# Two z1 tiles that stay on chip, an earlier load of the others, and small steps moved apart in a one-core gated mix of attention and gMLP

## The chip, the cores and the metric

The kernel runs on one core of a Trainium2 chip. A core has TensorE (PE: matmuls, with its own weight loads, PEld), VectorE (DVE), ScalarE (ACT), GpSimd (POOL) and SyncE (SP), each with an instruction stream of its own that it works off in order, and 16 DMA engines that serve the queues. An instruction waits on semaphores until what it reads is there and what it overwrites has been read. SBUF, the on-chip memory, has 128 partitions; PSUM, into which matmuls write, is used here as 8 banks of 512 f32 per partition. The metric is the device time of one execution in microseconds (us), median over runs.

## What is computed

x is 2048 x 1024, in bf16. Branch A is attention with 32 heads of 32: each position s looks at the 8 positions s, s-2, ..., s-14 of its own head. Branch B is a gMLP: a projection to 2 x 1792 columns, GELU, a layer norm of one half, a product with a 2048 x 2048 matrix over the positions, a product with the other half, and a projection back. A gate per position mixes them.

```
g = sigmoid((x * gate_w).sum(-1, keepdims=True))
qkv = x @ wqkv                                  # 32 heads of 32
logits = q . k[s - 2w], w = 0..7, * 32**-0.5    # positions below 0: -1e9
a = (softmax(logits) . v[s - 2w]) @ wo
z = gelu(x @ w_in);  z1, z2 = z[:, :1792], layernorm(z[:, 1792:])
b = (z1 * (w_sp @ z2 + b_sp[:, None])) @ w_out
out = g * a + (1 - g) * b
```

## The kernel before, in words

**Stages of TensorE**, one after the other (line of the matmul in brackets): part of z2 (L280), q, k and v (L516), the rest of z2 (L280), z1 (L591), the product with w_sp for the position chunks 0 and 1 (L605), the same for chunks 2 and 3 by seven products in place of eight (L696), the projections back, where w_out's products (L822) alternate with wo's (L899 for the first pair of row blocks, then L909, seven products in place of eight as well). Everything that those shortened schemes add and subtract is kept in range by powers of two, below.

**z1.** 14 tiles of 128 features (f) by 4 chunks of 512 positions (c). Each (f, c) takes 8 matmuls into one bank; ScalarE applies the GELU into a staging slot (`z1s`, two slots, taken in turn), and after four chunks SP stores the tile to DRAM (`z1_d`, L595). `load_z1c(0)` (L466) fetches chunk 0 with its 14 tiles into `z1c_slots[0]`; it is called after the z1 loop. Chunk 1 goes into `z1c_slots[1]`, which lies over the staging slots; chunks 2 and 3 are fetched tile by tile in the seven products (L710). `z1c_slots[0]` lies over the buffers of the "looks", below; the place of its tiles 12 and 13 does not.

**The w_sp products of chunks 0 and 1** (`g_chunk`). For each f, 16 matmuls into one bank, a ScalarE copy to one of three slots (L609), a bias added by VectorE (L612) and the product with z1 (L613), which is the first reader of the loaded z1.

**Attention** runs on VectorE beside all this, by 8 groups of 4 heads: products of q and k (L327) folded down (L330, L333, L338, L341), the maximum over the 8 windows by one `tensor_reduce` (L348) and the subtraction (L349), the exponential on ScalarE (L352), the sum over the windows by another `tensor_reduce` (L355), reciprocal (L356), weights (L357), the products with v (L365) and their folds (L371, L372, L368). The products with v of group g - 1 stand between the steps of group g. Loads of q, k and v per group and the store of the output (`store_o`, L383) are on SP's queue.

**The order of the work.** The engines' orders are written out at build time. A counter of planned time, `beat`, advances with each group of matmuls; what is registered with `beat.at(t, ...)` is emitted when the counter passes t, and the steps of attention are emitted by a plan that adds up durations given in the code (`yield t, 1.4, soft_a`). These times decide places in the order alone; on the chip an instruction runs when its engine has come to it and its waits are over.

**Looks and powers.** Sums of absolute values are taken of w_out (7 parts) and wo (4 parts): SP loads a part (L572) and ScalarE sums it (L574), during the z1 stage, planned every 8 us. From each set of sums a power of two is made by `whole_power`, in three turns: VectorE cuts the exponents (L546 to L549); TensorE transposes that column (L553) and VectorE takes its maximum (L554); TensorE spreads it over the partitions by a small matmul (L556) and VectorE forms the factors (L557 to L563). The turns of w_out's power are planned 70 us into the z1 stage, and 12 and 24 us into the w_sp stage; those of wo's at 42, 60 and 80 us.

**Rows of w_sp** 8 to 15 (128 rows each) are loaded on ScalarE's queue, summed (L625), scaled by powers of two per row (L662), stored to DRAM (`wsp_d`, L663) and read back transposed by SP (L463) in time for the seven products, whose sums t1 to t4 VectorE makes (L670 to L676). The scaled biases take a matmul (L653), a ScalarE copy (L655) and a store and load on SP.

**The first pair of row blocks** of the last stage (`mix_pair(0)`) is followed by `wo_scale` (L856), which scales all of wo by its power, by four sums of wo (L864 to L870) and by `attn_pair(0)` (L899). On VectorE, `mix_pair` has two steps near its end (L848, L850).

Of the kernel before, what the change touches and what calls it, by code (L numbers as in the profile page):

```python
# [15 lines left out]
P = 128  # L16
# [8 lines left out]
W = 8  # L25
# [32 lines left out]
def kernel(  # L58
# [78 lines left out]
    v_up = sm.tile([P, 1], I32, name="v_up")  # L137
    back = sm.tile([P, 1], I32, name="back")
    att_L = sm.tile([P, 2 * W * 8 * HG], F32, name="att_L")
    att_m = sm.tile([P, 2, 1, 32], F32, name="att_m")  # L140
    att_r = sm.tile([P, 2, 1, 32], F32, name="att_r")
    att_A = sm.tile([P, 2 * W * 8 * HG], BF, name="att_A")

# [174 lines left out]
    TT = nc.vector.tensor_tensor  # L318

    q4 = q_t.rearrange("p (n d) -> p n d", d=4)  # L320
    by_window = L4.rearrange("p a w n -> p a n w")

    def qk_steps(jh):
        def mul():
# [15 lines left out]
    def to_one():  # L340
# [3 lines left out]
        for t in range(3):  # L344
            nc.gpsimd.memset(_sub_ap(first, 128 + 32 * t, [[128, 2], [1, 24 - 8 * t]]), NEG)

    def soft_a():
        nc.vector.tensor_reduce(att_m[:, :, 0, :], by_window, AX.X, ALU.max)  # L348
        TT(L4, L4, att_m[:].to_broadcast([P, 2, W, 32]), ALU.subtract)  # L349

    def soft_exp():
        nc.scalar.activation(L[:], L[:], ACT.Exp, scale=float(SCALE))  # L352

    def soft_b():
        nc.vector.tensor_reduce(att_m[:, :, 0, :], by_window, AX.X, ALU.add)  # L355
        nc.vector.reciprocal(att_r[:], att_m[:])  # L356
        TT(A4, L4, att_r[:].to_broadcast([P, 2, W, 32]), ALU.mult)  # L357

    def pv_steps(g, jh):
# [30 lines left out]
    def attention_steps(t):  # L390
        beat.at(t - 8.0, lambda: load_qk(0))
        beat.at(t + 35.0, lambda: load_v(0))
        for g in range(NG):
            for took, fn in qk_steps(0) + qk_steps(1) + [(1.2, to_two), (1.1, to_one)]:
                yield t, took, fn
            t = beat.vector
            if g + 1 < NG:
                beat.at(t + 1.0, lambda g=g: load_qk(g + 1))
            if g == 0:
                t += 3.0  # L400
            else:
                for took, fn in pv_steps(g - 1, 0):
                    yield t, took, fn
                t = beat.vector
            yield t, 1.4, soft_a
            t = beat.vector
            beat.at(t + 1.0, soft_exp)
            if g == 0:
                t += 5.0
            else:  # L410
                for took, fn in pv_steps(g - 1, 1):
                    yield t, took, fn
                t = beat.vector
                if g + 1 < NG:
                    beat.at(t + 1.0, lambda g=g: load_v(g))
                else:
                    load_v(g)
                if g % 2 == 0:
                    beat.at(t + 1.5, lambda g=g: store_o(g - 1))
            yield t, 2.0, soft_b  # L420
            t = beat.vector
        for took, fn in pv_steps(NG - 1, 0) + pv_steps(NG - 1, 1):
            yield t + 5.0, took, fn
        t = beat.vector
        beat.at(t + 14.0, lambda: store_o(NG - 1))
# [37 lines left out]
        sync.dma_start_transpose(wsp_slots[c][:, :, aa, :], src)  # L463

    def load_z1c(c):
        sync.dma_start(z1c_slots[c % 2].rearrange("p f t -> p (f t)"), z1_d[c])  # L466

    tc_order = ctx.enter_context(tc.manual_schedule())

# [98 lines left out]
    for k in range(11):  # L568
        slot = look_slots[k % 2]
        src = wout_v[:, 2 * k:2 * k + 2, :] if k < 7 else wo_rows[:, 2 * k - 14:2 * k - 12, :]  # L570
        total = w_l1[:, k:k + 1] if k < 7 else wo_l1[:, k - 7:k - 6]
        beat.at(beat.now + 3.0 + 8.0 * k, lambda src=src, slot=slot: sync.dma_start(  # L572
            slot.rearrange("p (f n) -> p f n", f=2), src))
        beat.at(beat.now + 10.5 + 8.0 * k, lambda total=total, slot=slot: nc.scalar.activation(  # L574
            look_out, slot, ACT.Abs, accum_out=total))

    for g in range(NG):
        beat.at(beat.now + 6.0 + 10.0 * g, lambda g=g: turn_wo(g))
    w_steps = whole_power(w_up, omg[:])
    beat.at(beat.now + 70.0, lambda: (nc.vector.tensor_reduce(top[:], w_l1[:], AX.X, ALU.max), next(w_steps)))  # L580

    for f in range(NF):
        ch = f // 4
        w1 = w1_slots[ch % 2]
        if f % 4 == 0 and ch in (1, 2):
            load_w1(ch + 1)
        z1s = z1s_slots[f % 2]
        for c in range(4):
            ps = psum.tile([P, 512], F32, name="ps", tag="ps")
            for kt in range(KT):  # L590
                nc.tensor.matmul(ps[:], w1[:, kt, (f % 4) * P:(f % 4 + 1) * P], xT[:, kt, 512 * c:512 * (c + 1)],  # L591
                                 start=(kt == 0), stop=(kt == KT - 1))
            nc.scalar.activation(z1s[:, c, :], ps[:], ACT.Gelu_apprx_tanh)  # L593
            beat.run(KT * 512)
        sync.dma_start(z1_d[:, :, f * 512:(f + 1) * 512].rearrange("c p t -> p c t"), z1s)  # L595

    gs = [0]

# [159 lines left out]
    def w_tiles(f):  # L758
        return (w_out_sb[:, f, 0:512], w_out_sb[:, f, 512:1024],
                w_out_sb[:, f + 7, 0:512], w_out_sb[:, f + 7, 512:1024])  # L760
# [63 lines left out]
    def mix_slot(a, n0):  # L824
        return mix_slots[2 * (a % 4) + n0 // 512]

    def mix_pair(q):
        a, b = 2 * q, 2 * q + 1
        s = row_pair_sums[q % 2]
        og = [omg[:, r:r + 1] for r in (a, b)]  # L830
        stt = nc.vector.scalar_tensor_tensor
        act = nc.scalar.activation
        pa = bank()
        product7(pa, u_rows(q, 0, 0), lambda j: w_tiles(f_of(q, j))[0], True)
        pb = bank()
        nc.scalar.copy(pb[:], pa[:])
        pe = bank()
        product7(pe, s[0], lambda j: w_t(f_of(q, j), 0), True)
        for r in (1, 0):
            act(mix_slot(a + r, 512), pe[:], ACT.Copy, scale=og[r])  # L840
        product7(pb, s[1], lambda j: w_t(f_of(q, j), 1), False)
        pc = bank()
        nc.scalar.copy(pc[:], pb[:])
        product7(pa, u_rows(q, 0, 1), lambda j: w_tiles(f_of(q, j))[2], False)
        act(mix_slot(a, 0), pa[:], ACT.Copy, scale=og[0])
        o_scale(a)
        product7(pb, s[2], lambda j: w_t(f_of(q, j), 2), False)
        stt(mix_slot(b, 512), pb[:], og[1], mix_slot(b, 512), ALU.mult, ALU.add)  # L848
        product7(pc, s[3], lambda j: w_tiles(f_of(q, j))[3], False)
        stt(mix_slot(a, 512), pc[:], og[0], mix_slot(a, 512), ALU.mult, ALU.add)  # L850
        product7(pb, u_rows(q, 1, 1), lambda j: w_t(f_of(q, j), 3), False)
        act(mix_slot(b, 0), pb[:], ACT.Copy, scale=og[1])
        o_scale(b)

    def wo_scale():
        nc.vector.tensor_scalar(wo_sb, wo_sb, wo_up[:].bitcast(F32), None, ALU.mult)  # L856

    def wo_tiles():
        return wo_sb[:, 0:4, 0:512], wo_sb[:, 0:4, 512:1024], wo_sb[:, 4:8, 0:512], wo_sb[:, 4:8, 512:1024]
# [160 lines left out]
        for k in range(4):  # L1020
            u_sum(q, k)

    load_z1c(0)
    t0 = beat.now
    for r in range(8):
        beat.at(t0 + 3.5 * r, lambda r=r: natural(r))
# [21 lines left out]
    biases()  # L1048
    wo_steps = whole_power(wo_up, g_s[:])
    for k in range(2):  # L1050
        beat.at(t0 + 12.0 + 12.0 * k, lambda: next(w_steps))
        beat.at(t0 + 60.0 + 20.0 * k, lambda: next(wo_steps))
    beat.at(t0 + 42.0, lambda: (nc.vector.tensor_reduce(top[:], wo_l1[:], AX.X, ALU.max), next(wo_steps)))
    g_chunk(0)
    g_chunk(1)
    for n in range(7):
# [3 lines left out]
    u_steps = whole_power(u_up, omg[:, 8:16])  # L1060
    prepare(1)
    mix_pair(0)
    wo_scale()
    u_sums(6)
    for k in range(4):
        wo_sum(k)
# [38 lines left out]
```

## Time and profile before

| | us |
|---|---|
| runs | 701.94, 700.68, 703.32; median 701.94 |
| profiled execution, own time | 702.48 |
| its span | 700.4 |
| TensorE busy | 683.9 |
| VectorE, ScalarE busy | 531.5, 385.8 |
| mean granted TensorE clock | 0.993 |

Rows of the profile name a line, an engine, an operation and what it writes and reads. In a time line the first two columns are start and duration, and a bracket at the end gives the idle time of the engine ahead of the instruction and what ended it. In the view of waits the columns are total, number and longest. In the groups of instructions the columns behind the bar are busy time, mean duration in ns and idle time ahead. "SPq" is SP's queue at the issue of a DMA. `arena` is the one large SBUF buffer in which nearly all tiles lie, so a row's line tells more than its tile name; `z_d` is `z1_d`. Some matmul records are missing from a trace (439 of 448 in a group, for instance).

### The profile page before, as it was taken

What the parts mean: (1) busy time and instruction counts of PE and PEld (TensorE: products, weight loads), DVE (VectorE), ACT (ScalarE), POOL (GpSimd) and SP (SyncE); (2) the same over time, 40 slices, a digit from 0 to 9 for tenths busy, and PEclk for the clock granted to TensorE, in tenths of its full rate; (3) what the DMA queues carried; (4) which work ended last, traced back from release to release, by engine and by line L of the source; (5) the groups of instructions that cost most, each with busy time, mean ns of one, the idle gap of its engine ahead of it and who ended that gap; (6) DMA issues with size and microseconds to landing.
All of it is one profiled execution on the core that took longest, in us unless ns stands there. A gap on an engine that the chain in (4) does not pass through costs nothing.

```text
span 700.4 us, 8978 instructions
## 1 busy us (share of the span) xinstructions
PE 683.9 (98%) x3307; PEld 360.3 (51%) x3355; DVE 531.5 (76%) x652; ACT 385.8 (55%) x778; POOL 13.7 (2%) x44
## 2 busy tenths in 40 slices
PE   9999999999999999999999599999999989999998
PEld 4499666666665554444444244444444444444443
DVE  0004689999999999999993998267589998676663
ACT  4345544435568898666664797673665552232232
POOL 0000000000000101100000000000000000000000
PEclk9999999999999999999999799999999999999999
DMA  8996868768673233997777937946211323222220
GB/s 231 188 201 162 194 168 200 183 174 159 181 198 140 87 111 100 250 296 251 271 249 243 315 128 178 279 99 228 73 32 61 120 61 76 60 61 75 61 60 30
DMA packets 186923, 109.19 MB, mean 156 GB/s; under 512 B 145920, under 2 KB 171520, under 8 KB 186624
## 3 DMA queue, kind: packets, MB, share of 16 engines
q1 hardware_dynamic: 184576, 100.23, 53.2%
q10 hardware_dynamic: 2304, 8.39, 3.4%
q8 instruction: 26, 0.43, 0.2%
q14 instruction: 17, 0.14, 0.1%
HBM read 59.77 MB, written 34.67 MB: 135 GB/s over the span
## 4 chain that ended last, share of the span: by engine, by line
PE 81%; DMA 8%; ACT 4%; SPq 3%; DVE 2%; issue 2%; DVEq 0%; ACTq 0%
PE ps L516 24%; PE ps L280 14%; PE ps L696 12%; PE ps L822 12%; PE ps L605 11%; PE ps L909 6%; DMA z_d<-arena 4%; DMA arena<-in_B_w_out_dram 2%; PE ps L591 2%; SPq L463 2%; ACT arena L593 1%; ACT arena L574 1%; DMA arena<-z_d 1%; PE ps L899 1%; SPq L572 1%
## 5 line engine op out<-in xcount | busy, mean ns | idle before, releaser
L516 PE MATMUL ps<-arena 128*128 128x512 bf16 (+1 forms) x896 | 166.2, 349 | 0.0
L516 PEld LDWEIGHTS <-arena 128*128 128x128 bf16 x896 | 120.3, 144 | 45.8
L327 DVE TENSOR_TENSOR arena<-arena 128x8192 bf16<-128x8192 bf16 x16 | 70.7, 4421 | 56.2 <-DMA arena<-k_d 56.0
L519 ACT CAST arena<-ps 128x512 bf16<-128x512 f32 (+1 forms) x112 | 57.7, 526 | 85.7 <-PE ps L516 80.5
L605 PE MATMUL ps<-arena 128*128 128x512 bf16 x439 | 100.0, 387 | 0.5
L280 PE MATMUL ps<-arena 128*128 128x512 bf16 (+1 forms) x501 | 97.0, 352 | 1.4 <-DMA arena<-in_B_w_in_dram 0.7
L591 PE MATMUL ps<-arena 128*128 128x512 bf16 x439 | 96.4, 379 | 0.5
L822 PE MATMUL ps<-arena 128*128 128x512 f16 (+1 forms) x380 | 91.2, 379 | 0.5
L696 PE MATMUL ps<-arena 128*128 128x512 f16 (+1 forms) x385 | 84.7, 379 | 0.6 <-issue 0.3
L605 PEld LDWEIGHTS <-arena 128*128 128x128 bf16 x448 | 44.0, 99 | 61.7 <-issue 11.7
L280 PEld LDWEIGHTS <-arena 128*128 128x128 bf16 x512 | 50.0, 98 | 48.1 <-issue 1.3
L591 PEld LDWEIGHTS <-arena 128*128 128x128 bf16 x448 | 43.8, 98 | 52.7
L365 DVE TENSOR_TENSOR arena<-arena,att_A 128x8192 bf16<-128x8192 bf16 x16 | 70.7, 4418 | 0.0
L822 PEld LDWEIGHTS <-arena 128*128 128x128 f16 (+1 forms) x392 | 38.3, 98 | 46.1
L696 PEld LDWEIGHTS <-arena 128*128 128x128 bf16 (+1 forms) x392 | 38.0, 98 | 45.9 <-issue 0.5
L330 DVE TENSOR_TENSOR arena<-arena 128x4096 bf16<-128x4096 bf16 (+1 forms) x32 | 56.2, 1757 | 1.0
L909 PE MATMUL ps<-arena 128*128 128x512 f16 (+3 forms) x200 | 50.3, 375 | 0.1
L285 ACT ACTIVATE arena<-ps 128x512 bf16<-128x512 f32 (+1 forms) x64 | 34.3, 538 | 26.8 <-PE ps L280 26.7
L889 DVE SCALAR_TENSOR_TENSOR arena<-ps,g_s,arena 128x512 bf16<-128x512 f32 (+2 forms) x33 | 23.9, 733 | 29.9 <-ACT arena L941 20.0
L593 ACT ACTIVATE arena<-ps 128x512 bf16<-128x512 f32 x56 | 31.2, 595 | 25.5 <-DMA z_d<-arena 12.6
L371 DVE TENSOR_TENSOR arena<-arena 128x4096 bf16<-128x4096 bf16 x16 | 36.6, 2289 | 0.4
L909 PEld LDWEIGHTS <-arena 128*128 128x128 f16 (+1 forms) x200 | 19.4, 98 | 23.1 <-issue 0.2
(168 smaller groups left out, 627.3 us busy)
## 6 DMA issues: line engine op xcount, KB each, us to landing
arena<-k_d SPq DMA_DIRECT2D x8, 960.0 KB, 7.9
arena<-v_d SPq DMA_DIRECT2D x8, 960.0 KB, 6.0
z_d<-arena SPq DMA_DIRECT2D x14, 512.0 KB, 3.6
arena<-in_A_wqkv_dram SPq DMA_DIRECT2D x24, 256.0 KB, 4.1
arena<-in_B_w_in_dram SPq DMA_DIRECT2D x4, 1024.0 KB, 5.6
q_d<-arena SPq DMA_DIRECT2D x32, 128.0 KB, 2.4
k_d<-arena SPq DMA_DIRECT2D x32, 128.0 KB, 2.2
arena<-q_d SPq DMA_DIRECT2D x8, 512.0 KB, 4.6
```

The costliest lines, as they stand in the source:

```text
L280: nc.tensor.matmul(ps[:, 0:N], xT[:, kt, i * P:(i + 1) * P], w2[:, kt, ZC * c:ZC * c + N], start=(kt == 0), stop=(kt == KT - 1))
L327: TT(prod.rearrange("p (w j c) -> p w j c", w=W, j=8, c=C), in0, in1, ALU.mult)
L330: return lambda: TT(pv[:, :, 0:half], pv[:, :, 0:half], pv[:, :, half:2 * half], ALU.add)
L365: TT(prod.rearrange("p (w j d h) -> p w j d h", w=W, j=8, d=DH, h=HG), in0, in1, ALU.mult)
L516: nc.tensor.matmul(ps[:, n0:n1].rearrange("p (t c) -> p t c", c=C), lhsT, wgt[:, pos0:pos1, kt, :], start=(kt == 0), stop=(kt == KT - 1))
L519: nc.scalar.copy(st[:, j % 4, n0:n1], ps[:, n0:n1])
L591: nc.tensor.matmul(ps[:], w1[:, kt, (f % 4) * P:(f % 4 + 1) * P], xT[:, kt, 512 * c:512 * (c + 1)], start=(kt == 0), stop=(kt == KT - 1))
L593: nc.scalar.activation(z1s[:, c, :], ps[:], ACT.Gelu_apprx_tanh)
L605: nc.tensor.matmul(ps[:], z2[:, f, i, :], wsp[:, i, :, :].rearrange("p a t -> p (a t)"), start=(i == 0), stop=(i == 15))
L696: nc.tensor.matmul(dst[:], lhs[:, k, :], rhs(k), start=first and k == 0, stop=k == 7, skip_group_check=not first)
L822: nc.tensor.matmul(dst[:], lhs[:, j, :], rhs(j), start=first and j == 0, stop=j == 6, skip_group_check=not first)
L909: nc.tensor.matmul(dst, lhs[:, k, :], rhs[:, k, :], start=first and k == 0, stop=k == 3, skip_group_check=not first)
```

## The change

- **z1.** For tiles 12 and 13 the GELU of chunks 0 and 1 writes to its place in `z1c_slots[c]`, and only chunks 2 and 3 go through the staging slot and to DRAM. `load_z1c` fetches tiles 0 to 11. For chunk 0 it is called after the store of tile 12.
- **Looks** every 7 us of planned time instead of 8, from 2 us instead of 3.
- **Turns of the powers**: w_out's at 72 us into the z1 stage, then 14 and 32 us into the w_sp stage; wo's at 48, 66 and 84 us.
- **wo** is scaled in two halves of its columns; the first stands between the two late VectorE steps of `mix_pair`, the second where the whole stood.
- **Windows**: maximum and sum over 8 windows by three folds of 256, 128 and 64 elements instead of one `tensor_reduce`; the planned durations of some attention steps change with it.

In the order of instructions that comes out, w_out's transposition stands behind 5 tiles of the w_sp product (before: 4) and its spreading matmul behind 10 (before: 7); wo's behind 20 and 25 (before: 18 and 24); the scaled biases' matmul stands behind 19 in both. On VectorE the first L612 and L613 stand behind L365, L371 and L372 of group 6 (before: behind L365). On SP the store of the attention's last output stands ahead of the last four transposes from `wsp_d` (before: behind two of them).

```diff
-    att_m = sm.tile([P, 2, 1, 32], F32, name="att_m")
+    att_m = sm.tile([P, 2, 4, 32], F32, name="att_m")
...
+    def windows(op):
+        TT(att_m[:], L4[:, :, 0:4, :], L4[:, :, 4:8, :], op)
+        TT(att_m[:, :, 0:2, :], att_m[:, :, 0:2, :], att_m[:, :, 2:4, :], op)
+        TT(att_m[:, :, 0:1, :], att_m[:, :, 0:1, :], att_m[:, :, 1:2, :], op)
+
     def soft_a():
-        nc.vector.tensor_reduce(att_m[:, :, 0, :], by_window, AX.X, ALU.max)
-        TT(L4, L4, att_m[:].to_broadcast([P, 2, W, 32]), ALU.subtract)
+        windows(ALU.max)
+        TT(L4, L4, att_m[:, :, 0:1, :].to_broadcast([P, 2, W, 32]), ALU.subtract)
...
     def soft_b():
-        nc.vector.tensor_reduce(att_m[:, :, 0, :], by_window, AX.X, ALU.add)
-        nc.vector.reciprocal(att_r[:], att_m[:])
+        windows(ALU.add)
+        nc.vector.reciprocal(att_r[:], att_m[:, :, 0:1, :])
...
-            for took, fn in qk_steps(0) + qk_steps(1) + [(1.2, to_two), (1.1, to_one)]:
+            for took, fn in qk_steps(0) + qk_steps(1) + [(0.7, to_two), (0.7, to_one)]:
...
-            yield t, 1.4, soft_a
+            yield t, 1.65, soft_a
...
-            yield t, 2.0, soft_b
+            yield t, 2.2, soft_b
...
     def load_z1c(c):
-        sync.dma_start(z1c_slots[c % 2].rearrange("p f t -> p (f t)"), z1_d[c])
+        sync.dma_start(z1c_slots[c][:, 0:12, :].rearrange("p f t -> p (f t)"), z1_d[c, :, 0:12 * 512])
...
-        beat.at(beat.now + 3.0 + 8.0 * k, lambda src=src, slot=slot: sync.dma_start(
+        beat.at(beat.now + 2.0 + 7.0 * k, lambda src=src, slot=slot: sync.dma_start(
             slot.rearrange("p (f n) -> p f n", f=2), src))
-        beat.at(beat.now + 10.5 + 8.0 * k, lambda total=total, slot=slot: nc.scalar.activation(
+        beat.at(beat.now + 9.5 + 7.0 * k, lambda total=total, slot=slot: nc.scalar.activation(
             look_out, slot, ACT.Abs, accum_out=total))
...
-    beat.at(beat.now + 70.0, lambda: (nc.vector.tensor_reduce(top[:], w_l1[:], AX.X, ALU.max), next(w_steps)))
+    beat.at(beat.now + 72.0, lambda: (nc.vector.tensor_reduce(top[:], w_l1[:], AX.X, ALU.max), next(w_steps)))
...
-            nc.scalar.activation(z1s[:, c, :], ps[:], ACT.Gelu_apprx_tanh)
+            keep = f > 11 and c < 2
+            nc.scalar.activation(z1c_slots[c][:, f, :] if keep else z1s[:, c, :], ps[:], ACT.Gelu_apprx_tanh)
             beat.run(KT * 512)
-        sync.dma_start(z1_d[:, :, f * 512:(f + 1) * 512].rearrange("c p t -> p c t"), z1s)
+        c0 = 2 if f > 11 else 0
+        sync.dma_start(z1_d[c0:4, :, f * 512:(f + 1) * 512].rearrange("c p t -> p c t"), z1s[:, c0:4, :])
+        if f == 12:
+            load_z1c(0)
...
         stt(mix_slot(b, 512), pb[:], og[1], mix_slot(b, 512), ALU.mult, ALU.add)
+        wo_scale(0)
         product7(pc, s[3], lambda j: w_tiles(f_of(q, j))[3], False)
         stt(mix_slot(a, 512), pc[:], og[0], mix_slot(a, 512), ALU.mult, ALU.add)
...
-    def wo_scale():
-        nc.vector.tensor_scalar(wo_sb, wo_sb, wo_up[:].bitcast(F32), None, ALU.mult)
+    def wo_scale(h):
+        half = wo_sb[:, :, 512 * h:512 * h + 512]
+        nc.vector.tensor_scalar(half, half, wo_up[:].bitcast(F32), None, ALU.mult)
...
-    load_z1c(0)
     t0 = beat.now
...
     for k in range(2):
-        beat.at(t0 + 12.0 + 12.0 * k, lambda: next(w_steps))
-        beat.at(t0 + 60.0 + 20.0 * k, lambda: next(wo_steps))
-    beat.at(t0 + 42.0, lambda: (nc.vector.tensor_reduce(top[:], wo_l1[:], AX.X, ALU.max), next(wo_steps)))
+        beat.at(t0 + 14.0 + 18.0 * k, lambda: next(w_steps))
+        beat.at(t0 + 66.0 + 18.0 * k, lambda: next(wo_steps))
+    beat.at(t0 + 48.0, lambda: (nc.vector.tensor_reduce(top[:], wo_l1[:], AX.X, ALU.max), next(wo_steps)))
...
     mix_pair(0)
-    wo_scale()
+    wo_scale(1)
```

The changed file's lines are shifted: L556 becomes L560, L613 becomes L621, L696 becomes L704, L899 becomes L909, for instance.

More of the change, by code (lines that the diff above doesn't have):

```diff
@@ L320 @@
     q4 = q_t.rearrange("p (n d) -> p n d", d=4)
-    by_window = L4.rearrange("p a w n -> p a n w")
     def qk_steps(jh):
```

## The prediction

> **What bounds the kernel now.** I read the page first, then who waited for whom, then time lines around the waits of TensorE (PE). The page:
>
> ```profile
> span 700.4 us, 8978 instructions
> ...
> PE 683.9 (98%) x3307; PEld 360.3 (51%) x3355; DVE 531.5 (76%) x652; ACT 385.8 (55%) x778; POOL 13.7 (2%) x44
> ...
> PE   9999999999999999999999599999999989999998
> ```
>
> TensorE is the bound nearly everywhere, so only its holes are to be had. Two slices stand out: the 23rd (about 385 to 402 us), half idle, and the 33rd. The waits name their holes, and the time lines of TensorE, VectorE (DVE) and SP's queue show how the first comes about:
>
> ```profile
> PE po L556 <- DVE top L554: 7.1, 1, 7.1
> ...
> PE ps L899 <- ACT arena L852: 1.7, 1, 1.7
> ```
>
> ```profile
> 269.18 96.86 PE L591 MATMUL ps<-arena 128*128 128x512 bf16 x439
> ...
> 366.07 13.99 PE L605 MATMUL ps<-arena 128*128 128x512 bf16 x63
> ...
> 397.81 0.58 PE L556 MATMUL po<-top,const-bfloat16-1.0 1*128 1x512 bf16 x1 [7.14 <-DVE top L554]
> ```
>
> ```profile
> 474.64 1.67 PE L696 MATMUL ps<-arena 128*128 128x512 bf16 x7
> ```
>
> ```profile
> 368.03 4.42 DVE L365 TENSOR_TENSOR arena<-arena,att_A 128x8192 bf16<-128x8192 bf16 x1
> 372.53 0.42 DVE L612 TENSOR_TENSOR arena<-arena 128x512 bf16<-128x512 bf16 x1
> 384.64 0.42 DVE L613 TENSOR_TENSOR arena<-arena 128x512 bf16<-128x512 bf16 x1 [11.69 <-DMA arena<-z_d]
> 384.98 2.28 DVE L371 TENSOR_TENSOR arena<-arena 128x4096 bf16<-128x4096 bf16 x1
> ...
> 388.05 1.22 DVE L372 TENSOR_TENSOR arena<-arena 128x2048 bf16<-128x2048 bf16 x1
> 389.30 0.69 DVE L368 TENSOR_TENSOR arena<-arena 128x1024 bf16<-128x1024 bf16 x1
> ...
> 397.48 0.27 DVE L554 TENSOR_REDUCE top<-po 1x1 bf16<-1x128 bf16 x1
> ```
>
> ```profile
> 376.51 0.33 SPq L466 DMA_DIRECT2D arena<-z_d  x1
> ```
>
> The chain is this. The load of chunk 0's z1 (L466) stands behind the store of the last z1 tile; it starts at 376.51 and arrives at 384.6. VectorE sits 11.69 us in the middle of attention behind the first product with z1. The one-row reduction L554 of w_out's power is queued behind that on VectorE and ends at 397.75, and TensorE, in order, has the small matmul L556 in front of its next tile: 7.14 us idle. The granted clock then stays down (stretches of time: their length, busy time of the five engines, then the clock, the share of the DMA engines, GB/s):
>
> ```profile
> 390.70:397.80 7.10, 0.00 (x0) 0.00 (x0) 7.03 (x8) 5.18 (x12) 0.00 (x0) 0.70 1.05 296
> 397.80:404.00 6.20, 6.19 (x15) 2.04 (x15) 6.06 (x9) 6.01 (x17) 0.00 (x0) 0.52 0.98 403
> ...
> 366.00:372.00 6.00, 6.00 (x30) 2.79 (x30) 5.93 (x4) 5.97 (x17) 0.38 (x4) 1.00 0.05 5
> ```
>
> 6.20 us at 0.52 lose 6.2 x 0.48 = 3.0 us. Cross-check: 56 groups of 8 matmuls took 96.86 us (L591), 1.73 each, so a g tile of 16 takes 3.46 and 28 tiles 96.9. With some 1.3 us for the small matmuls among them the stage would last 98.2; it lasted 474.64 - 366.07 = 108.6. The 10.4 us too much are the 7.14 and some 3.2 of slow clock.
>
> **The change, part by part.**
>
> Early z1 and spread powers. In the changed order the load of chunk 0 (12 of 14 tiles) stands behind the store of tile 12 and waits for the stores up to tile 11 and the last look at wo, not for tile 13. TensorE finishes tile 12 near 269.2 + 13 x 6.92 = 359.1, so it is issued near 360. The latest sign of tile 11's store:
>
> ```profile
> 364.82 0.60 ACT L593 ACTIVATE arena<-ps 128x512 bf16<-128x512 f32 x1 [4.39 <-DMA z_d<-arena]
> ```
>
> If it lands as late as that, the load starts at 364.8. It took 8.1 us for 14 tiles, 6.9 for 12: landing by 371.7 at the worst, partly inside the 6 us (366 to 372, quoted above) in which the DMA engines now stand idle. VectorE asks for it later than before: the first pair of g steps is now placed behind three steps of attention, 368.0 + 4.4 + 2.3 + 1.2 = 375.9. Margin 4 us, so the 11.69 us wait goes. Behind the load on SP's queue stand the store of tile 13 and the four transposes of w_sp for chunk 1, which wait for TensorE's last z1 matmul (366.0) and no more for the load's issue at 376.5: they start some 10 us earlier.
>
> w's transpose now follows 5 g tiles instead of 4 and its matmul 10 tiles instead of 7, at 366.1 + 34.6 + 0.3 = 401. VectorE has until then 18.2 us of attention (L365, L371, L372 twice, L368, a fold and a subtraction) and 5 pairs L612, L613 of 0.85: L554 (after: L558) is done at 368.0 + 22.5 + 0.3 = 390.8, 10 us ahead. If the load arrived no earlier than before (384.6), it would be 8.7 us later, 399.5, still ahead of 401. Each half of this edit alone nearly covers the stall. Gain 7.14 + 3.0 to 3.2; I take 10.3. What is late next: below, first rival.
>
> [...]
>
> wo in halves.
>
> ```profile
> L806 DVE TENSOR_SCALAR arena<-arena,v_up 128x3584 bf16<-128x3584 bf16 x4 | 4.6, 1145 | 0.0
> L767 DVE TENSOR_SCALAR arena<-arena,w_up 128x1024 bf16<-128x1024 bf16 x14 | 6.1, 479 | 0.0
> L856 DVE TENSOR_SCALAR arena<-arena,wo_up 128x8192 bf16<-128x8192 bf16 x1 | 2.3, 2341 | 0.0
> ```
>
> ```profile
> 568.44 0.75 DVE L848 SCALAR_TENSOR_TENSOR arena<-ps,omg,arena 128x512 f32<-128x512 f32 x1 [0.26 <-PE ps L822]
> 569.95 0.75 DVE L850 SCALAR_TENSOR_TENSOR arena<-ps,omg,arena 128x512 f32<-128x512 f32 x1 [0.76 <-PE ps L822]
> 570.61 2.34 DVE L856 TENSOR_SCALAR arena<-arena,wo_up 128x8192 bf16<-128x8192 bf16 x1
> ```
>
> ```profile
> 560.60 10.74 PE L822 MATMUL ps<-arena 128*128 128x512 bf16 x48
> 573.05 7.07 PE L899 MATMUL ps<-arena 128*128 128x512 bf16 x32 [1.72 <-ACT arena L852]
> ```
>
> The view blames ScalarE (ACT) for the 1.72 us, but L852 ended at 572.07; the wait ends when wo is scaled, 570.61 + 2.34 = 572.95. Half of wo is 4096 wide: between the rows for 3584 and 8192, 1.28 us; at worst, as four of the 1024 rows, 1.92. The first half now starts behind L848 at 569.1 and ends at 570.4 (571.0), before TensorE is free at 571.34. L850 follows 0.4 (1.1) later than now, the second half ends at 572.4 (573.6), and TensorE needs it at 571.34 + 1.73 = 573.07. Gain 1.72, at worst 1.2. The sums of wo behind it start no later than now (or 0.6 later); their first use is more than 5 us on.
>
> Windows as three folds.
>
> ```profile
> L348 DVE TENSOR_REDUCE att_m<-att_L 128x64 f32<-128x512 f32 x8 | 8.4, 1046 | 0.5 <-POOL att_L L345 0.5
> L349 DVE TENSOR_TENSOR att_L<-att_L,att_m 128x512 f32<-128x512 f32 x8 | 5.5, 692 | 0.3
> ...
> L441 DVE TENSOR_TENSOR var<-mean 128x4 f32<-128x4 f32 x4 | 0.6, 161 | 0.1
> ```
>
> Between 161 ns for 4 and 692 ns for 512 elements, folds of 256, 128 and 64 take 0.42 + 0.29 + 0.22 = 0.94 us against 1.05: 16 times 0.1, VectorE 1.7 us shorter, about nothing with the small gaps of two more instructions. On the path neither counts: VectorE is 10 us ahead where TensorE next waits for it. (wo's three turns are moved apart too; TensorE has no wait at them now.)
>
> Looks at the weights every 7 us instead of 8, their loads past SP's stores by as much: nothing, hidden under L591, which ran 96.86 us without a hole although ScalarE, in order, waited up to 4.39 us for a store (row above). Eight PSUM banks of 1.73 us cover some 12 us. If that cover is gone, TensorE waits (second rival). The halved stores of tiles 12 and 13 move 1 MB less to and fro, off the path.
>
> The sum: the profiled execution took 702.48 (span 700.4), 0.5 above the median of 701.94. 702.48 - 10.3 - 1.7 = 690.5; against the median, 690.0, which I predict. With the worse end of wo's term (1.2) it is 690.5.
>
> **The rivals.** First, the stall moves on to the start of the seven products.
>
> ```profile
> 464.50 2.29 DVE L670 TENSOR_TENSOR arena<-arena 128x4096 f16<-128x4096 bf16 x1
> ...
> 473.83 2.28 DVE L674 TENSOR_TENSOR arena<-arena 128x4096 f16<-128x4096 bf16 x1
> ```
>
> ```profile
> 449.57 0.61 SPq L383 DMA_DIRECT2D o_d<-arena  x1
> 450.23 8.35 SPq L463 DMA_TRANSPOSE arena<-wsp_d  x2
> ```
>
> The sums t1 to t2 (L670 to L674) are ready at 476.1 and the third product asks for t2 at 474.64 + 2 x 1.73 = 478.1: 2 us of slack, and TensorE comes 10.3 us sooner. They rest on the transposed w_sp, those on rows that ScalarE scales, and on SP on b_row, which TensorE's own L653 sets:
>
> ```profile
> 392.51 1.28 ACT L352 ACT_TABLE_LOAD   x1 [3.85 <-DVE att_L L349]
> ...
> 441.61 2.00 ACT L662 ACTIVATE arena<-arena,up 128x2048 bf16<-128x2048 bf16 x1
> ...
> 444.56 0.25 ACT L655 CAST b_row<-pt 8x128 bf16<-8x128 f32 x1
> ```
>
> Against it: ScalarE's run from the exponential to the last scaled row takes 443.6 - 392.5 = 51.1 us. It now starts behind the subtraction of head group 7, at 368.0 + 11.1 = 379.1 (the steps above), with one set of four row sums (3 us) more in it: end near 433.2, 10.4 sooner, and L653 moves with TensorE. So the chain moves as far as TensorE does. If it moves 4 to 8 us less, 2 to 6 us come back past the slack: 692 to 696. (The hole of 1.72 us cost no clock, 32 matmuls in 7.07 us behind it; that of 7.14 cost 3.0.)
>
> The other side, slower: in the new order the 1 MB store of the attention's last output stands ahead of all four of these transposes, now (L383) ahead of the last two. If the chain to t2 doesn't move at all and the store puts it 4 us later (1 MB at the pace of the z1 load), TensorE waits 478.1 - 10.3 to 480.1: 12.3 us, and loses 3 us of clock, against 12.0 gained: 706. It decides when t2 is ready after about 477 on the old time scale.
>
> Second, ScalarE falls behind in the z1 stage. The looks now come at the period of an f tile (6.9 us). With waits like the longest here in three or four periods running, the backlog passes 12 us and TensorE stops for 2 to 5 us: 692 to 697. Against it: a look waited so long only once.
>
> ```profile
> ACT arena L574 <- DMA arena<-in_A_wo_dram: 4.4, 1, 4.4
> ```
>
> Third, the change doesn't do it: the load lands past 386 among w_sp's transposes and VectorE comes late to L558 after all; only wo's 1.7 us and a little remain, 699 to 701.
>
> **How the numbers follow.** Forecast 0.72 (own range 688.5 to 691.5, the spread of the runs shown, 700.68 to 703.32, laid about it); first rival in part 0.11; second 0.06; these are faster, 0.89. Third 0.05: within 0.5% (3.5 us, about what a measurement tells from no change). Slower 0.06. The range of 8 in 10 takes the first two rivals to 696.5 and begins at 688.5.
>
> **What would show it.** Right: no wait of DVE L621 for z_d above 1 us; the early load lands before 376; L560 and L909 without a wait; granted clock 1.00 from 385 to 410; the first L704 near 464; the span near 688. Wrong: a hole of PE at the start of L704, in L595, or still at L560.

## The result, and the profile after

The changed kernel took 690.87 us (median of four executions, 689.91 to 691.45) beside 702.12 us of the kernel before (four, 700.68 to 703.32): a ratio of 0.984, 95% interval 0.982 to 0.986. The forecast was 690.0. Six more executions in a later comparison gave a median of 690.70, with one of the six at 696.73; the experiments come back to that one.

The profiled execution took 691.45 us. The page of the changed kernel (span and instructions, busy time by engine, TensorE's busy tenths in 40 slices):

```profile
span 689.4 us, 9052 instructions
...
PE 683.3 (99%) x3355; PEld 359.1 (52%) x3355; DVE 530.3 (77%) x685; ACT 385.9 (56%) x778; POOL 12.6 (2%) x44
...
PE   8999999999999999999999999999999999999998
```

The slice that stood at 5 is full. TensorE's list of waits is now complete in two rows, neither of which is at a power's small matmul or at the first product with wo:

```profile
PE ps L280 <- DMA arena<-in_B_w_in_dram: 2.1, 3, 1.3
PE pw L100 <- PEq L1098: 0.8, 1, 0.8
```

TensorE's time line (start, length, line, what it does): the z1 stage, w_out's two small matmuls L557 and L560, the start of the seven products (L704), and the first product with wo (L909):

```profile
270.15 96.86 PE L595 MATMUL ps<-arena 128*128 128x512 bf16 x448
...
384.42 0.22 PE L557 MATMUL po<-ident,top_b 128*1 128x128 bf16 x1
...
401.94 0.38 PE L560 MATMUL po<-top,const-bfloat16-1.0 1*128 1x512 bf16 x1
...
465.52 14.84 PE L704 MATMUL ps<-arena 128*128 128x512 bf16 x68
...
562.06 7.07 PE L909 MATMUL ps<-arena 128*128 128x512 bf16 x32
```

From the start of z1 (269.18 before, 270.15 now) to the seven products (474.64, 465.52) it is 195.37 us in place of 205.46, 10.1 less; from there to the first product with wo (573.05, 562.06) 96.54 in place of 98.41, 1.9 less; what follows is equal. The sum is 12.0. This execution began z1 0.97 us later, because the first loads of w_in came later (2.1 us of waits above), so the spans differ by 11.0. In the stretch in which the clock stood at 0.52 before, it is now full (length, busy time of the five engines, clock, DMA share, GB/s):

```profile
385.00:398.00 13.00, 13.00 (x62) 5.92 (x61) 9.24 (x22) 12.39 (x35) 0.00 (x0) 1.00 1.05 392
398.00:410.00 12.00, 12.00 (x56) 5.24 (x55) 10.47 (x16) 10.42 (x23) 0.00 (x0) 1.00 0.23 91
```

The chain that carried the loss, SP's queue first (its row of three stores, then the third of them by itself), then ScalarE, then VectorE:

```profile
355.97 9.08 SPq L601 DMA_DIRECT2D z_d<-arena  x3
365.22 0.65 SPq L470 DMA_DIRECT2D arena<-z_d  x1
```

```profile
364.69 0.36 SPq L601 DMA_DIRECT2D z_d<-arena  x1
```

```profile
362.97 0.60 ACT L598 ACTIVATE arena<-ps 128x512 bf16<-128x512 f32 x1 [4.75 <-DMA z_d<-arena]
```

```profile
374.50 0.42 DVE L620 TENSOR_TENSOR arena<-arena 128x512 bf16<-128x512 bf16 x1
375.00 0.43 DVE L621 TENSOR_TENSOR arena<-arena 128x512 bf16<-128x512 bf16 x1
...
388.70 0.27 DVE L558 TENSOR_REDUCE top<-po 1x1 bf16<-1x128 bf16 x1
```

The product with z1, which waited 11.69 us as L613, waits for nothing as L621, and the reduction L558 is done 13.0 us ahead of TensorE. The load was issued at 365.22, behind the store of tile 12, which went out only at 364.69: the last GELUs of that tile had waited 4.75 us for an earlier store to land and free the staging slot. By the last of its completion events in the trace the load landed at 372.3, 7.1 us after its issue and 2.7 us before L621 read it.

### The profile page after: what moved, and what is told of

It is laid out like the page before. It is cut to its first block, busy times and chain, and to the rows that moved or that the text cites. A ratio compares the mean times of both kernels' runs of the same rounds, so it can differ in the third digit from the quotient of the medians.

```text
span 689.4 us, 9052 instructions
## 1 busy us (share of the span) xinstructions
PE 683.3 (99%) x3355; PEld 359.1 (52%) x3355; DVE 530.3 (77%) x685; ACT 385.9 (56%) x778; POOL 12.6 (2%) x44
## 4 chain that ended last, share of the span: by engine, by line
PE 98%; DMA 1%; SPq 0%; ACT 0%; DVE 0%; issue 0%; DVEq 0%
PE ps L520 24%; PE ps L613 14%; PE ps L595 14%; PE ps L280 14%; PE ps L704 12%; PE ps L830 12%; PE ps L919 6%; PE ps L909 1%; DMA arena<-in_B_w_in_dram 1%; PE po L560 0%; SPq L477 0%; SPq L475 0%; PE po L557 0%; ACT arena L973 0%; DVE arena L899 0%; SPq L479 0%
## 5 line engine op out<-in xcount | busy, mean ns | idle before, releaser
L520 PE MATMUL ps<-arena 128*128 128x512 bf16 (+1 forms) x896 | 166.2, 349 | 0.0
L280 PE MATMUL ps<-arena 128*128 128x512 bf16 (+1 forms) x512 | 97.6, 352 | 2.1 <-DMA arena<-in_B_w_in_dram 2.1
L613 PE MATMUL ps<-arena 128*128 128x512 bf16 x448 | 97.7, 379 | 0.0
L830 PE MATMUL ps<-arena 128*128 128x512 f16 (+1 forms) x392 | 92.8, 379 | 0.0
L704 PE MATMUL ps<-arena 128*128 128x512 bf16 (+1 forms) x392 | 85.5, 379 | 0.0
L613 PEld LDWEIGHTS <-arena 128*128 128x128 bf16 x448 | 43.3, 98 | 52.3 <-issue 0.7
L704 PEld LDWEIGHTS <-arena 128*128 128x128 bf16 (+1 forms) x392 | 38.0, 98 | 45.9 <-issue 0.5
L899 DVE SCALAR_TENSOR_TENSOR arena<-ps,g_s,arena 128x512 bf16<-128x512 f32 (+2 forms) x33 | 23.9, 733 | 28.5 <-ACT arena L951 20.0
```

The costliest lines, as they stand in the source:

```text
L280: nc.tensor.matmul(ps[:, 0:N], xT[:, kt, i * P:(i + 1) * P], w2[:, kt, ZC * c:ZC * c + N], start=(kt == 0), stop=(kt == KT - 1))
L520: nc.tensor.matmul(ps[:, n0:n1].rearrange("p (t c) -> p t c", c=C), lhsT, wgt[:, pos0:pos1, kt, :], start=(kt == 0), stop=(kt == KT - 1))
L613: nc.tensor.matmul(ps[:], z2[:, f, i, :], wsp[:, i, :, :].rearrange("p a t -> p (a t)"), start=(i == 0), stop=(i == 15))
L704: nc.tensor.matmul(dst[:], lhs[:, k, :], rhs(k), start=first and k == 0, stop=k == 7, skip_group_check=not first)
L830: nc.tensor.matmul(dst[:], lhs[:, j, :], rhs(j), start=first and j == 0, stop=j == 6, skip_group_check=not first)
```

## The experiments

All are edits of the changed kernel, and times stand against its 690.7 to 690.9. In the two that take the load back, the lines from there on are 4 lower (L616, L617, L609, L678, L700 for L620, L621, L613, L682, L704).

**The turns as before, the early load kept (e1_turns_back, e1_again).**

```
-    beat.at(beat.now + 72.0, ... next(w_steps)))
+    beat.at(beat.now + 70.0, ... next(w_steps)))
...
-        beat.at(t0 + 14.0 + 18.0 * k, lambda: next(w_steps))
-        beat.at(t0 + 66.0 + 18.0 * k, lambda: next(wo_steps))
+        beat.at(t0 + 12.0 + 12.0 * k, lambda: next(w_steps))
+        beat.at(t0 + 60.0 + 20.0 * k, lambda: next(wo_steps))
...
-    beat.at(t0 + 48.0, ... next(wo_steps)))
+    beat.at(t0 + 42.0, ... next(wo_steps)))
```

> The changed kernel with the powers' turns as they were (w_out's transpose after 4 g tiles, its matmul after 7; wo's at 42, 60 and 80 us), the early load of chunk 0 kept. My theory, that either half of the edit alone covers the stall at w_out's power: the one-row reduction L558 stands behind 4 pairs of g steps on VectorE and ends near 387, TensorE's small matmul L560 is reached near 391.4, so no wait, clock 1.00 throughout, and the time of the changed kernel, 690.9 us (690 to 692). The rival, that the spread turns carry the gain: L560 waits 2 to 5 us, clock down behind it, 695 to 699 us.

Six executions: 690.09, 690.56, 691.13, and 695.76, 698.08, 699.08, the last three with a mean granted clock of 0.994 to 0.997. The profiled one is the fastest. VectorE and TensorE in it:

```profile
385.34 0.27 DVE L558 TENSOR_REDUCE top<-po 1x1 bf16<-1x128 bf16 x1
```

```profile
390.19 0.39 PE L560 MATMUL po<-top,const-bfloat16-1.0 1*128 1x512 bf16 x1
```

The reduction is 4.6 us ahead, no wait, and the time is that of the changed kernel: in this execution the early load alone removes the stall. But half of the executions lose 5 to 9 us somewhere, with the clock down in part. By time and clock they would fit the rival; whether it was L560 that waited in them, this profile cannot say. It was profiled once more:

> One more profile of the kernel with the turns as before and the early load, of which three of six executions took 695.8 to 699.1 us. If this one is among the slow: my theory is that w_sp's four transposes took over 20 us, VectorE's L369 waited more than 6 us for v, and TensorE waits in or before L704 with the clock at 0.5 for one or two stretches of 3.4 us behind it; the rival, that L560 of w_out waits near 390 because the early load landed late. If it is among the fast, near 690.5, it tells nothing on this.

It took 691.13, without a hole, so where the late three wait was not seen.

**The z1 path as before, the turns kept apart (e2_load_back).** The store and `load_z1c` take all fourteen tiles again, in lines not shown here.

```
-            keep = f > 11 and c < 2
-            nc.scalar.activation(z1c_slots[c][:, f, :] if keep else z1s[:, c, :], ...)
+            nc.scalar.activation(z1s[:, c, :], ...)
...
-        if f == 12:
-            load_z1c(0)
...
+    load_z1c(0)
     t0 = beat.now
```

> The changed kernel with chunk 0's z1 path as it was (all fourteen tiles stored and loaded, the load issued after the last store), the turns kept apart. In both theories VectorE waits some 10 us for the load (it arrives near 384.6, asked for at 375.0), its reduction L558 ends near 398.3, and TensorE reaches L560 only at 401.9: no hole there. Theory A (the prediction's sentence that each half alone nearly covers the stall, and that the transposed w_sp does not hang on the load): nothing is late behind it, 691 to 693 us. Theory B (the first rival): the exponential of head group 7 stands behind the subtraction behind the waiting g step, so ScalarE's row sums and scaled rows come 6 to 9 us later, t2 is ready at 472 to 475 and the third product asks for it at 469: a hole of 3 to 6 us in L704 with 0 to 3 us of clock behind it, 694 to 700 us. I now hold B the likelier; my value is 696.

695.82 us (694.47 to 698.24). In the profiled execution, the slowest of the four, L617 waits 12.37 us for the load, L558 ends at 400.06, 0.7 us before TensorE's L560: no hole there. TensorE's waits are these:

```profile
PE ps L700 <- DVE arena L687: 2.7, 1, 2.7
PE po L557 <- DVE top_b L553: 1.8, 1, 1.8
PE ps L700 <- DVE arena L678: 1.7, 1, 1.7
```

Theory B: VectorE's lateness passes through the exponential (ScalarE's L356 waited 11.8 us for it) to the scaled rows and to t2, whose sum L678 is done at 475.68 where the third product would have been reached at 469.7. A second delay adds to it: the four transposes of w_sp start 7.4 us later than in the changed kernel's profile (378.45 and 371.04), the load of the last head group's v stands behind them on SP's queue, and VectorE waits 5.84 us for it (2.69 there). The first scaled row starts 8.8 us later than there and the last 9.95. 6.2 us of holes and 1.4 of slow clock make most of the 7.9 by which the stretch from z1 to the first product with wo is longer. So when only the turns are moved, TensorE stalls at the start of the seven products instead (4.4 of the 6.2 us) and, less, at the transposition of wo's power.

**Both taken back (e3_both_back)**, the two diffs above together.

> The changed kernel with both taken back (late load and the turns close together), leaving the halves of wo, the three folds and the looks every 7 us. My theory: the stall of the kernel before comes back, L558 ends near 396.5 and TensorE is at L560 near 391.4: a hole of 5 to 7 us and 3 us of slow clock behind it, 699 to 701 us, that is, the early load and the turns together are worth 8 to 10 us. The rival, that a good part of the gain came from the folds, the looks or the halved stores: 692 to 697 us.

697.94 us (696.35 to 701.25), 7.1 above the changed kernel, between the ranges of the two theories.

```profile
396.35 0.58 PE L560 MATMUL po<-top,const-bfloat16-1.0 1*128 1x512 bf16 x1 [6.07 <-DVE top L558]
```

The old stall is back at the old place, but 1.1 us shorter than the 7.14 of before and with 1.8 us of slow clock in place of 3.0. The load lands as before (384.43, before 384.64), but from there to the reduction VectorE has 11.59 us of work, 12.84 before: other steps of attention stand between. These 2.3 us and wo's 1.7 make most of the 4.2 that this kernel has over the one before.

**wo scaled whole (e4_wo_whole).**

```
-        wo_scale(0)
...
-    wo_scale(1)
+    wo_scale()
```

> The changed kernel with wo scaled whole in one instruction at the old place. My theory: L909 waits 1.7 us as before, the clock stays at 1.00, 692.6 us (ratio to the changed kernel 1.0025). The rival, that the hole is smaller or hidden on this shorter path, or that other work moves into it: 690.9 us, no wait above 0.5 at L909.

692.57 us (five of six 692.08 to 694.02, one 698.34): 1.7 to 1.9 more. L907 waits 1.72 us, the clock stays full (1.00). The profiled execution, 694.02, has a second wait, which the changed kernel's profile has not, and its cause is in the trace, on SP's queue, VectorE and TensorE:

```profile
369.93 24.24 SPq L467 DMA_TRANSPOSE arena<-in_B_w_sp_dram  x4
```

```profile
405.62 4.43 DVE L369 TENSOR_TENSOR arena<-arena,att_A 128x8192 bf16<-128x8192 bf16 x1 [8.98 <-DMA arena<-v_d]
```

```profile
469.66 29.53 PE L704 MATMUL ps<-arena 128*128 128x512 f16 x136 [1.80 <-DVE arena L682]
```

The four transposes of w_sp took 24.24 us here, 15.61 in the changed kernel's profile. The last head group's v is loaded behind them on the same queue, attention waits 9 us for it, and t2 is 1.8 us late. That made a theory of the late executions, tried next.

**The changed kernel again, and v on another queue (after_again, e8_v_act, e9_turns_v).** e8 is the changed kernel, e9 the one with the turns as before, both with this edit:

```
-    def load_v(g):
-        sync.dma_start(v_t, ...)
+    def load_v(g, queue=sync):
+        queue.dma_start(v_t, ...)
...
                 else:
-                    load_v(g)
+                    load_v(g, nc.scalar)
```

> The changed kernel once more, to see how far its executions spread beside those of the experiments. My theory: it keeps 2 to 3 us of slack at t2 and 8 to 13 us at the powers' matmuls, so it stays within 689.9 and 691.5 in most executions; where w_sp's four transposes take 24 us in place of 15, as in the profiled run with wo scaled whole, t2 is 1 to 2 us late and an execution shows 692 to 693. The rival, that the scatter of the run with the turns taken back (690.1 to 699.1) belongs to the early load and is there in the changed kernel too: some executions above 695.

> The changed kernel with one edit: the load of the last head group's v goes out on ScalarE's queue, behind the first four row sums (near 384.5), and not on SP's behind the four transposes of w_sp and the second z1 load. My theory: VectorE's L369 no longer waits (2.7 us in the changed kernel's profile, 9.0 with the long transposes), and since nothing on TensorE hangs on that wait in an ordinary execution the median stays at 690.9 us (690.2 to 691.5), the highest execution no higher than 692. The rival, that the load now shares the DMA engines with the transposes and lengthens them: t2 late, 692 to 694 us.

> The kernel with the powers' turns as before and the early load, and the same edit for v. Without the edit three of its six executions took 695.8 to 699.1 us, the others 690.1 to 691.1. Theory A, that in those three the four transposes held v back, VectorE waited up to 9 us for it and one of wo's turns (its transpose at 428.6, its matmul at 450.0) or t2 was late: now all executions within 690 and 692 us. Theory B, that in those three the early z1 load itself landed late and w_out's reduction L558 (ready 4.8 us before TensorE asked for it in the profiled one) missed its turn: the scatter stays, about half of the executions above 695 us with the mean clock at 0.994 to 0.997.

The changed kernel again: 690.06 to 690.90 in five executions, and 696.73 in one, as its rival had it. e8: 690.30 (690.15 to 690.93). e9: 690.81 (689.93 to 691.30), none of five late, where three of seven were without the edit. The load went out at 386.1 in e8 and its wait was 1.1 us, as in the profile of the changed kernel beside it, whose transposes took 14.2 us that time and whose load went out at 385.3, so here the other queue made no difference; in e9 the wait was none. Over both kernels no execution of nine is late with v on ScalarE's queue, and 4 of 17 are with v on SP's. This is what theory A says, on too few executions to call it settled. Against theory B: in the ten profiles of kernels with the early load and the quicker looks, that load landed 2.1 to 3.0 us before L621 read it; but none of these ten is of a late execution. e8's median is 0.4 us below the changed kernel's, within their scatter: a guard against the late ones if anything, not a faster kernel.

**Two of the transposes twice (e12_more_transposes, e11_turns_transposes)**, in the changed kernel and in the one with the turns as before:

```
-    for aa in range(4):
+    for aa in (0, 1, 2, 3, 0, 1):
         load_wsp(1, aa)
```

> The changed kernel with the first two of w_sp's four transposes for chunk 1 issued a second time behind the fourth, so that the second z1 load and the load of v on the same queue come some 8 us later, as in the profiled run with wo scaled whole, where the four took 24.2 us by themselves. My theory: VectorE's L369 waits 8 to 10 us for v, the scaled rows and t2 come 4 to 6 us later, the third of the seven products waits 1.5 to 3 us, 692.5 to 695 us. The rival, that the wait for v is covered and long transposes do not explain executions near 696: 690 to 691.5 us.

> The same two more transposes in the kernel with the powers' turns as before (early load kept). Theory A, that the spread turns guard against a late v: VectorE comes to wo's reduction late, TensorE waits at wo's transpose (428.6) or its matmul (450.0) besides t2, and with slow clock behind it the time is 695 to 699 us, 2 us or more above the same with the turns apart. Theory B, that only t2 is late and the turns' distance is nothing to it: within 1 us of the other.

e12: 690.98 us, four executions at 690.45 to 691.11, two at 694.33 and 695.40. e11: 694.36, three at 690.76 to 691.90, three at 696.81 to 698.27. Neither profile is of a late execution, and in both VectorE waits 8.6 us for v. e12 at t2:

```profile
465.65 2.28 DVE L682 TENSOR_TENSOR arena<-arena 128x4096 f16<-128x4096 bf16 x1
```

```profile
464.73 32.97 PE L704 MATMUL ps<-arena 128*128 128x512 bf16 x150
```

t2 is done at 467.93, and the third product is reached at 464.73 + 2 x 1.73 = 468.19: 0.3 us are left of the 2.7 in the changed kernel's profile (466.28 and 468.98). With a wait for v of 1.2 us (e1's profile) 2.7 are left, with 4.5 (e1_again) 1.4, with 8.6 (e11) 0.5, with 9.0 and the longer transposes (e4) it is 1.8 short. So the wait of 8 us for v is covered, against my forecast of 692.5 to 695, but it takes the cover away, and what else comes late in an execution is then paid: two or three of six. The late executions are 2 to 3 us later in e11 than in e12; wo's transpose L557 has 3.4 us of slack there in the profile and 5.9 in e12, which would fit theory A, and in e2, where VectorE is later still, TensorE does wait there. But no late execution of these kernels was profiled, and the place of the wait in them stays open.

**Small and large holes (e6_two_holes).**

```
-        beat.at(t0 + 14.0 + 18.0 * k, lambda: next(w_steps))
-        beat.at(t0 + 66.0 + 18.0 * k, lambda: next(wo_steps))
+        beat.at(t0 + 14.0 + 0.5 * k, lambda: next(w_steps))
+        beat.at(t0 + 66.0 + 0.5 * k, lambda: next(wo_steps))
```

> The changed kernel with the small transpose and the small matmul of each of the two powers put back to back, so that TensorE waits for VectorE's reduction in between: at w_out's near 384.5 (L558 done near 389: a hole of about 4.4 us) and at wo's near 437.5 (L558 done near 438.9: a hole of about 1.5 us). Theory A (a hole costs itself, and behind one of several us the granted clock is low for a time, as behind the 7.14 us of the kernel before, while one of 1.5 us costs no clock): 5.9 us of holes and 1.5 to 3 us of clock behind the first alone, 698 to 700 us. Theory B (no clock is lost behind a hole under 5 us): 696.5 to 697 us, clock 1.00 behind both.

698.90 us (ten executions, 698.07 to 699.62). The holes are 4.37 and 1.64 us, and from z1 to the seven products it takes 8.6 us more than in the changed kernel: 2.6 of clock, all behind the first hole (theory A). Behind the second the clock is full (1.00). The stretches at half clock, in the order kernel before (hole 7.14), e3 (6.07), e6 (4.37) and e2 (2.73):

```profile
393.60:403.80 10.20, 5.99 (x14) 1.94 (x14) 10.03 (x13) 9.90 (x28) 0.00 (x0) 0.50 1.02 385
```

```profile
393.10:400.00 6.90, 3.65 (x9) 1.16 (x9) 6.73 (x13) 6.71 (x19) 0.00 (x0) 0.51 1.08 332
```

```profile
387.00:393.70 6.70, 5.37 (x12) 1.79 (x13) 4.73 (x17) 0.10 (x2) 0.00 (x0) 0.50 0.95 391
...
445.30:449.00 3.70, 3.67 (x17) 1.58 (x17) 1.07 (x7) 1.68 (x6) 0.00 (x0) 1.00 1.03 233
```

```profile
471.20:474.60 3.40, 2.84 (x7) 0.73 (x5) 3.37 (x6) 0.52 (x1) 0.00 (x0) 0.50 0.33 90
```

The lengths are three, two, two and one times the last row's 3.4 us, to within 0.1 us. What is lost is half of the busy time in them (first number behind the length): 3.0, 1.8, 2.7, 1.4.

**The folds and the looks as before (e10_small_back).**

```
-        TT(att_m[:], L4[:, :, 0:4, :], L4[:, :, 4:8, :], op)
-        ... two more folds
+        nc.vector.tensor_reduce(att_m[:, :, 0, :], by_window, AX.X, op)
...
-        beat.at(beat.now + 2.0 + 7.0 * k, ...)
-        beat.at(beat.now + 9.5 + 7.0 * k, ...)
+        beat.at(beat.now + 3.0 + 8.0 * k, ...)
+        beat.at(beat.now + 10.5 + 8.0 * k, ...)
```

> The changed kernel with the two edits that the prediction priced at nothing taken back together: the reduce over the windows in place of the three folds, and the looks at the weights every 8 us. My theory: 690.8 us (690.0 to 691.5), no new wait of TensorE; VectorE's busy time 1 to 2 us longer. The rival, that the looks' period or VectorE's 1 to 2 us hold up the early load (its issue waits for the last look and for the stores) or the chain to t2: 692 to 695 us.

697.94 us (eleven executions, 694.42 to 702.42, and one at 689.93). Neither theory's size. The last look at wo is planned 90.5 us into the stage and the early load at 13 x 6.92 = 90.0, and the looks use the memory of chunk 0's z1. So the look now stands behind the load, reads z1 for wo, and writes over four of the loaded tiles: that part of the computation is changed. In time, ScalarE waits for the load:

```profile
369.93 1.91 ACT L578 ACTIVATE arena<-arena 128x2048 bf16<-128x2048 bf16 x1 [7.24 <-DMA arena<-z_d]
```

Behind it the stores of z1 and the casts of g are late, w_sp's transposes start at 376.44 (371.04), v is waited for 6.9 us at 411.45, and TensorE waits 1.4 us at wo's transpose and 2.6 and 3.0 us in L704, with half clock for 3.4 us behind the last. The 16 reduces take 16.8 us, the 48 folds 15.0; what this alone does to the time the run doesn't tell, since the looks hide it. It was not tried by itself.

## Why the prediction was right, and where its steps were not

The sum came out: 12.0 us of holes and clock predicted, 12.0 measured between the same marks of the two profiles.

**Early z1 and spread turns, 10.3:** 10.1 between the profiles. But the edit taken back by itself (e3) costs 7.1. The rest of the change had shortened the old stall by 1.1 us and its clock by 1.2, as less of attention stood ahead of the reduction. The prediction gave the whole stall to one edit and nothing to the others; the total hides this, since the stall goes as a whole either way.

**"Each half of this edit alone nearly covers the stall":** right at L560, where the reduction is 4.6 us early with the load alone and 0.7 with the turns alone (1.5 forecast). As a statement on the time it fails for the turns: e2 loses 5.0 us, in its profile at the first sums of the seven products, t2 among them, and at wo's transpose. The step at fault asked only whether the reduction is in time at L560. The chain to t2 moves with VectorE's wait for z1, by way of the exponential, as the working of the first rival has it for the whole change, and with the load of v; without the early load neither moves. With the whole change both move, so nothing showed: the last scaled row ended at 434.5 (433.2 forecast), t2 has 2.7 us (2 before).

**The load's margin, 4 us:** 2.7. The load was issued at 365.22, not near 360 but close to the worst case of 364.8, and for the reason given there, a store that lands late; it took 7.1 us (6.9 forecast); and VectorE read at 375.0, not 375.9. The transposes of w_sp behind it started 5.9 us earlier than before (371.04 and 376.89), not some 10, since the store of tile 13 ahead of them went out at 370.58.

**First rival, in part:** seen at its place in the profiles of e2, e4 and e10, and perhaps in the one late execution of ten of the changed kernel (696.73, just above its 692 to 696), of which there is no profile. The prediction counted that the transposes start sooner, but not that v stands behind them on the queue, nor that their time varies.

**wo in halves, 1.72:** 1.72 by the hole and 1.7 to 1.9 by the medians (e4). The half took 1276 ns (L866), 1.28 forecast.

**Folds:** 418, 292 and 225 ns (0.42, 0.29, 0.22 forecast), VectorE as a whole 1.2 us shorter (1.7 forecast for the folds). That they are off the path was read from the 13 us at L560, not tried alone.

**The looks, "nothing":** right for z1, which still takes 96.86 us without a hole, and wrong as the price of the edit. The quicker looks free the memory and ScalarE for the early load; without them (e10) only 4 of the 11 us are gained, wo's halves among them. The prediction named the last look as one of the things the load waits for, and did not ask which of the two came first.

**The clock, 3.0 to 3.2:** right for the profiled execution: of the 10.2 us at 0.50 in the kernel before TensorE worked 5.99, half of which is 3.0, and in the changed kernel the clock is 1.00 there. Over the four stretches above the loss was 1.4 to 3.0 us, by their length (3.4 to 10.2 us) and by how much of it TensorE worked (2.84 to 5.99 us).

## What to carry to other kernels

A load that is moved forward takes along what is queued behind it (here w_sp's four transposes, 5.9 us earlier): follow each of those transfers to its consumer, and count the slack at the next place where the bounding engine waits, over several executions and not in one. When a wait on an engine is removed, ask which other chains hung on it; here two of them crossed, and the turns alone mostly moved the stall from one to the other. And a part of a change that costs nothing may still be what another part stands on: look for memory that both use.

## What the runs showed of the hardware

The clock's price came in steps here. The half clock (0.50) lasted 3.4, 6.7, 6.9 and 10.2 us behind holes of 2.73, 4.37, 6.07 and 7.14 us, and behind holes of 1.64 to 1.80 (e2, e4, e6) the clock stood at 1.00. The clock did not fall with the start of the hole, but 2.8 to 3.2 us after it, in e2 only 0.4 us after work had resumed. In the 3.4 us (the shortest stretch) that ended with the fall TensorE was idle for 2.7 to 3.2 us in all four.

In e10 a hole of 2.55 us cost no clock; one of 3.03 us, 1.9 us later, was followed by 3.4 us at half clock (the stretch of work ahead of it, the hole, and two stretches behind, where 1.60 x 0.35 + 3.00 x 0.38 = 1.7 us of clock are missing, half of 3.4):

```profile
470.50:472.40 1.90, 1.87 (x8) 0.67 (x8) 1.90 (x4) 0.00 (x0) 0.00 (x0) 1.00 0.00 0
472.40:475.40 3.00, 0.00 (x1) 0.01 (x1) 2.97 (x4) 0.58 (x1) 0.00 (x0) 1.00 0.72 222
475.40:477.00 1.60, 1.60 (x5) 0.62 (x6) 1.56 (x4) 0.00 (x0) 0.00 (x0) 0.65 0.90 274
477.00:480.00 3.00, 3.00 (x10) 1.19 (x9) 1.94 (x1) 0.57 (x1) 0.00 (x0) 0.62 0.94 304
```

In the 3.4 us ahead of the clock's return TensorE was idle for 0.56 us in e2, 0.22 in e6 and not at all in the other three. In the 3.4 us before these, with the clock at half, it was idle for 0.8 us (the kernel before), 1.1 (e6) and 3.2 (e3). Two holes of nearly one length came out differently (2.55 in e10: none; 2.73 in e2: 3.4 us at half clock). What decides this, and the length of the stretch, was not shown.

The same four transposes of w_sp on SP's queue took 14.1 to 24.2 us from one profile to the next, with the same code ahead of them in most, and 14.5 and 17.8 in two profiles of one kernel (e1), in which the order on the queue was the same.
